# Tokens 0 to 511 in rows of 128, the first x tile and DFT block in halves, and VectorE normalising for all four early tiles

## The chip, the cores and the metric

The kernel runs on one core of a Trainium2 chip. The metric is device time in microseconds (us). All times of a trace count from the start of the profiled span.

## The reference

`x` has 2048 tokens of 512 features. It is normalised by layer norm; of the result a two-dimensional Fourier mixing and a gated linear unit are computed; the two are multiplied, after a silu on the second.

```python
xn = _layernorm(A_x)                                    # (1, 2048, 512)
a, b = xn @ dft_hid_re.T, xn @ dft_hid_im.T
s = dft_seq_re @ a - dft_seq_im @ b                     # 2048x2048 each
h = _sigmoid(xn @ w_gate) * (xn @ w_up)                 # 512 -> 1792
return A_x + s * _silu(h @ w_down)                      # 1792 -> 512
```

## The kernel before

**Arithmetic.** Every matrix product is made of fp32r matmuls on a high and a low part of each operand. ScalarE (ACT) copies a raw page into the high part (`Parts.high`, L118), VectorE (DVE) subtracts it from the raw page to get the low part (`Parts.make`, L123), and `mm3` (L70) issues three matmuls for one product: high x high, and the two mixed ones. On top of that the large products are cut into 2x2 blocks and done with seven block products in place of eight; the sums for it are DVE work (`combine`, L127).

**Units.** The work of TensorE (PE) is a list of units. The first 24 are the only ones the change touches directly: for k = 1 and 2, for four token tiles pp = 0 to 3, for three chunks t = 0 to 2 of 512 output rows of the sequence DFT, one unit `Chunk.run(k, pp)` of 12 matmuls of 128x512. Units 0 to 11 have k = 1, units 12 to 23 k = 2; in each group units 0 to 2 are tile 0, 3 to 5 tile 1, and so on. Chunk t writes the PSUM banks `ga`/`ua`, `gb`/`ub` or `gc`/`uc`, so the names in the rows tell the chunk. Each unit needs its own DFT block (a page of 128x1024 fp32, 512 KB, from `in_c_re`), split in two parts, and half of the token tile (128x512), normalised and split in two parts, which three units share.

**A token tile.** `fetch(j, pp)` loads a page with 256 of a block of 512 tokens; j = 0 serves k = 1, and j = 1 serves k = 2. `stats(j, pp)` takes mean and variance on DVE (L160, L161), adds epsilon there, raises to the power -0.5 on GpSimd (POOL, L164 or L167) and multiplies to a bias on POOL (L173). `normalise(j, pp, d)` applies scale and bias on ACT in place (L179): `d = 0` or `1` is one half of the features, no `d` the whole page. For tiles 0 and 1 of j = 0 `begin` does it another way (`prepare`): the powers are taken for one token of the pair at a time (`apart`), and DVE subtracts the mean and multiplies by the power (`normed`, L392), ACT splits the half at once (`high`, L395), DVE makes the low part (`low`, L398).

**Order.** The order on each engine is the order in which the program issues. Before unit n come the calls registered with `sooner(n, ...)`, then loads up to 5 units ahead, then the splits of the operands up to 2 units ahead, then `amid(n, ...)`, the unit's matmuls, and `after(n, ...)`. `begin` issues the very first work by hand: 15 matmuls on ones that warm up PE, the first loads, and the splits for the first units. All loads go through SP's queue.

Much later, `x_norm` (L457) applies the stored means and scales to the transposed x for the gated unit, 512 tokens at a time, on DVE; its operand is read from DRAM, where `store_moments` put it.

Of the kernel before, what the change touches and what calls it, by code (L numbers as in the profile page):

```python
# [32 lines left out]
def fnet_glu_kernel(ctx: ExitStack, tc: tile.TileContext, x, x_t, c_re, c_im, w_h, w_gu, w_down, out):  # L33
# [115 lines left out]
    def fetch(j, pp):  # L149
        xs[j, pp] = page([2, D], F32)  # L150
        rows = x[pp * SB : (pp + 1) * SB, :].rearrange("(p j e) d -> p j e d", j=2, e=2)[:, j]
        nc.sync.dma_start(xs[j, pp], rows)

    def stats(j, pp, apart=None):
        mv = stat.tile([P, 2, 2], F32, name="mv")
        rs = stat.tile([P, 2], F32, name="rs")
        mean, scale, bias = (moments[:, pp, m, j, :] for m in range(3))
        for e in range(2):
            st = stat.tile([P, 6], F32, name="st")
            nc.vector.bn_stats(st, xs[j, pp][:, e, :])  # L160
            nc.vector.bn_aggr(mv[:, e, :], st)  # L161
            if apart:
                nc.vector.tensor_scalar(rs[:, e : e + 1], mv[:, e, 1:2], EPS, None, op0=ALU.add)
                nc.gpsimd.tensor_tensor(scale[:, e : e + 1], rs[:, e : e + 1], mhalf[:, e : e + 1], op=ALU.pow)  # L164
        if not apart:
            nc.vector.tensor_scalar(rs, mv[:, :, 1], EPS, None, op0=ALU.add)
            nc.gpsimd.tensor_tensor(scale, rs, mhalf, op=ALU.pow)  # L167
        if apart:
            apart(mv, 0)
        nc.vector.tensor_scalar(mean, mv[:, :, 0], -1.0, None, op0=ALU.mult)  # L170
        if apart:
            apart(mv, 1)
        nc.gpsimd.tensor_tensor(bias, mean, scale, op=ALU.mult)  # L173
        return mv

    def normalise(j, pp, d=None):
        for e in range(2):
            v = xs[j, pp][:, e, :] if d is None else a_block(d, j, pp)[:, e]
            nc.scalar.activation(v, v, AF.Identity, scale=moments[:, pp, 1, j, e : e + 1], bias=moments[:, pp, 2, j, e : e + 1])  # L179

    def store_moments(b):
        nc.gpsimd.dma_start(m_part[b], moments[:, b, 0:2].rearrange("p m j e -> p m (j e)"))
# [45 lines left out]
    class Chunk:  # L228
# [34 lines left out]
        def run(self, k, pp):  # L263
# [4 lines left out]
            order = [(d, e) for d in range(2) for e in range(2)]  # L268
            if (k, pp) == (1, 0) and self.t < TOGETHER:
                order.sort(key=lambda v: v[1])  # L270
            split_up = self.t < TOGETHER and k in (1, 2)
            for lows in ((0,), (1,), (2,)) if split_up else ((0, 1, 2),):
                for d, e in order:
                    ws = [v[:, e, d * P : (d + 1) * P] for v in wv]
                    first, last = k in (1, 5) and pp == e == 0, pp == 3 and e == 1
                    mm3(self.ps[ch, d], ws, [v[:, e, :] for v in xv], first, last, k not in (1, 5), self.t > 0 or (k < 3 and pp > 0), lows)
# [52 lines left out]

    def begin_seq():  # L330
# [34 lines left out]
    def begin(chunks):  # L365
        for i, tag in enumerate(("gb", "ub", "pd", "pd")):
            idle = bank(tag)
            for _ in range((4, 4, 4, 3)[i]):
                nc.tensor.matmul(idle, ones[:, :P], ones, start=True, stop=True)
        c = chunks[0].op[1, 0]  # L370
        raw = c.loads[0]
        fetch(0, 0)
        raw.load()
        for n in (1,):
            units[n][0][1].load()
        fetch(0, 1)
        for n in (2, 3, 4):
            units[n][0][1].load()
        fetch(0, 2)
        for n in (5,):  # L380
            units[n][0][1].load()
        c.at = page([2, SB]), page([2, SB])

        def tile_of(pp):
            a = aop[1, pp]
            both = page([2, 2, D // 2])
            a.at = both[:, 0], both[:, 1]
            return a.at, a_block(0, 0, pp)

        def normed(pp, mv, e):  # L390
            v = a_block(0, 0, pp)[:, e]
            nc.vector.tensor_scalar(v, v, mv[:, e, 0:1], moments[:, pp, 1, 0, e : e + 1], op0=SUB, op1=ALU.mult)  # L392

        def high(parts, src, e):
            nc.scalar.activation(parts[0][:, e], src[:, e], AF.Copy)  # L395

        def low(parts, src, e=slice(0, 2)):
            nc.vector.tensor_tensor(parts[1][:, e], src[:, e], parts[0][:, e].bitcast(F32), op=SUB)  # L398

        def prepare(pp, between):  # L400
            parts, src = tile_of(pp)

            def step(mv, e):
                normed(pp, mv, e)
                high(parts, src, e)
                between(e)

            stats(0, pp, step)
            return parts, src
# [37 lines left out]
    def x_norm(h, b, at):  # L447
# [448 lines left out]
def _layout(inputs):  # L896
    import numpy as np

    def seq(c):
        c = np.asarray(c).reshape(NT, SB, 4, P, 2, 2)  # L900
        return np.ascontiguousarray(c.transpose(0, 4, 2, 3, 5, 1))
# [41 lines left out]
```

## Time and profile before

| | |
|---|---|
| runs of the kernel | 803.99, 804.27, 808.01 us; median 804.27 us |
| the profiled execution | 803.3 us, of which the span is 801.5 us |
| PE | 790.1 us busy (99%), 3471 matmuls |
| DVE | 686.5 us busy (86%) |
| ACT | 513.1 us busy (64%) |
| POOL | 119.2 us busy (15%) |
| granted TensorE clock | 1.00 |

A row of the timeline has the start, the duration, engine, line, operation, output and input, and how many equal instructions it merges; in brackets stand the engine's idle time just before it and what ended that. A row of the windows has busy time and, in brackets, the number of instructions of each engine in that stretch. A row of the waits has the total, the number of waits and the longest one.

### The profile page before, as it was taken

What the parts mean: (1) busy time and instruction counts of PE and PEld (TensorE: products, weight loads), DVE (VectorE), ACT (ScalarE), POOL (GpSimd) and SP (SyncE); (2) the same over time, 40 slices, a digit from 0 to 9 for tenths busy, and PEclk for the clock granted to TensorE, in tenths of its full rate; (3) what the DMA queues carried; (4) which work ended last, traced back from release to release, by engine and by line L of the source; (5) the groups of instructions that cost most, each with busy time, mean ns of one, the idle gap of its engine ahead of it and who ended that gap; (6) DMA issues with size and microseconds to landing.
All of it is one profiled execution on the core that took longest, in us unless ns stands there. A gap on an engine that the chain in (4) does not pass through costs nothing.

```text
span 801.5 us, 9883 instructions
## 1 busy us (share of the span) xinstructions
PE 790.1 (99%) x3471; PEld 650.3 (81%) x3471; DVE 686.5 (86%) x899; ACT 513.1 (64%) x785; POOL 119.2 (15%) x161
## 2 busy tenths in 40 slices
PE   8999999999999999999999999999999999999997
PEld 6777888888888888888887887888888888888886
DVE  6789999878899798899999967869688898896957
ACT  5686665525434555677777866666577787887571
POOL 1330001000110000001211111222131111112201
PEclk9999999999999999999999999999999999999999
DMA  9944047288799336228976976799999798999996
GB/s 352 418 176 157 27 156 291 79 311 292 264 377 383 105 110 202 84 113 213 205 130 98 178 162 190 248 267 245 240 262 212 158 228 228 223 291 309 299 333 106
DMA packets 49185, 174.72 MB, mean 218 GB/s; under 512 B 5488, under 2 KB 5744, under 8 KB 49136
## 3 DMA queue, kind: packets, MB, share of 16 engines
q0 software_dynamic: 20320, 70.28, 39.7%
q1 hardware_dynamic: 28736, 103.76, 35.4%
q8 instruction: 27, 0.44, 0.2%
q14 instruction: 22, 0.18, 0.1%
q10 hardware_dynamic: 80, 0.07, 0.0%
HBM read 106.95 MB, written 70.80 MB: 222 GB/s over the span
## 4 chain that ended last, share of the span: by engine, by line
PE 85%; DVE 5%; issue 4%; DMA 3%; ACT 1%; POOL 1%; POOLq 0%; DVEq 0%; ACTq 0%
PE pd L70 25%; PE ga L70 15%; PE ua L70 15%; PE gc L70 10%; PE uc L70 10%; PE gb L70 5%; PE ub L70 5%; DMA g_part<-page 2%; DVE page L123 2%; DVE page L127 1%; DVE st L160 1%; ACT page L118 1%; DMA page<-in_x_dram 1%; POOL g_part L499 1%; ACT page L179 0%
## 5 line engine op out<-in xcount | busy, mean ns | idle before, releaser
L123 DVE TENSOR_TENSOR page<-page 128x1024 fp32r<-128x1024 f32 (+1 forms) x383 | 348.1, 940 | 63.6 <-ACT page L118 61.6
L118 ACT ACTIVATE page<-page 128x1024 fp32r<-128x1024 f32 (+1 forms) x383 | 302.3, 830 | 143.1 <-DVE page L127 122.5
L70 PE MATMUL pd<-page 128*128 128x512 f32 (+1 forms) x984 | 238.0, 387 | 0.0
L70 PEld LDWEIGHTS pd<-page 128*128 128x128 f32 x984 | 183.2, 188 | 37.5
L127 DVE TENSOR_TENSOR page<-page 128x1024 f32<-128x1024 f32 (+2 forms) x252 | 204.5, 834 | 2.5 <-DMA page<-in_w_gu_dram 1.5
L70 PE MATMUL ga<-page 128*128 128x512 f32 x600 | 156.6, 391 | 2.6 <-ACT page L395 1.2
L70 PE MATMUL ua<-page 128*128 128x512 f32 x600 | 155.5, 389 | 0.0
L70 PEld LDWEIGHTS ga<-page 128*128 128x128 f32 x600 | 112.1, 188 | 29.3 <-ACT page L395 2.2
L70 PEld LDWEIGHTS ua<-page 128*128 128x128 f32 x600 | 112.7, 188 | 23.4
L70 PE MATMUL gc<-page 128*128 128x512 f32 x408 | 106.8, 389 | 0.0
L70 PE MATMUL uc<-page 128*128 128x512 f32 x408 | 106.7, 389 | 0.0
L499 POOL DMA_DIRECT2D g_part<-page x76 | 65.4, 861 | 277.2 <-ACT page L508 160.8
L508 ACT ACTIVATE page<-pd 128x512 f32<-128x512 f32 x140 | 81.7, 599 | 25.5 <-PE pd L70 18.1
L70 PEld LDWEIGHTS gc<-page 128*128 128x128 f32 x408 | 76.5, 188 | 16.1 <-DVE page L123 0.2
L70 PEld LDWEIGHTS uc<-page 128*128 128x128 f32 x408 | 76.6, 188 | 15.9
L70 PE MATMUL gb<-page 128*128 128x512 f32 x228 | 61.3, 391 | 1.7 <-DVE page L123 1.7
L70 PE MATMUL ub<-page 128*128 128x512 f32 x228 | 61.0, 389 | 0.0
L70 PEld LDWEIGHTS gb<-page 128*128 128x128 f32 x228 | 42.5, 188 | 11.7 <-DVE page L123 3.1
L70 PEld LDWEIGHTS ub<-page 128*128 128x128 f32 x228 | 42.8, 188 | 8.9
L281 POOL DMA_DIRECT2D f_raw<-page x16 | 8.7, 542 | 207.8 <-DVE page L293 145.8
L634 DVE TENSOR_TENSOR page<-page 128x512 f32<-128x512 f32 x28 | 19.3, 690 | 8.7 <-ACT page L631 7.9
L594 DVE TENSOR_TENSOR page<-page,pd 128x512 f32<-128x512 f32 x28 | 18.5, 684 | 6.9 <-PE pd L70 6.9
(86 smaller groups left out, 352.3 us busy)
## 6 DMA issues: line engine op xcount, KB each, us to landing
g_part<-page POOLq DMA_DIRECT2D x84, 512.0 KB, 6.9
page<-in_c_re_dram SPq DMA_DIRECT2D x48, 512.0 KB, 8.2
page<-in_c_im_dram SPq DMA_DIRECT2D x32, 512.0 KB, 6.7
page<-f_raw SPq DMA_DIRECT2D x28, 512.0 KB, 7.8
page<-in_w_gu_dram SPq DMA_DIRECT2D x22, 512.0 KB, 6.7
f_raw<-page POOLq DMA_DIRECT2D x16, 512.0 KB, 5.1
f_sum<-page POOLq DMA_DIRECT2D x16, 512.0 KB, 7.3
page<-f_sum SPq DMA_DIRECT2D x16, 512.0 KB, 12.3
```

Of the source, the lines that this page charges most:

```text
L70: nc.tensor.matmul(ps, ws[w], ms[m], start=first and i == 0, stop=last and i == 2, skip_group_check=go_on)
L118: nc.scalar.activation(self.parts[0], self.raw, AF.Copy)
L123: nc.vector.tensor_tensor(lo, self.raw, hi.bitcast(F32), op=SUB)
L127: (engine or nc.vector).tensor_tensor(dst, a, b, op=op)
L160: nc.vector.bn_stats(st, xs[j, pp][:, e, :])
L281: nc.gpsimd.dma_start(f_raw[self.t][block], v)
L499: nc.gpsimd.dma_start(g_part[i], pg, accum_op=ADD)
L508: nc.scalar.activation(pg[:, o, :], po, AF.Copy, scale=float(sign))
L594: nc.vector.tensor_add(self.part[:, o, :], self.part[:, o, :], ps)
L634: nc.vector.tensor_mul(s[k][:, 0, :], s[k][:, 0, :], ps["u" + tag] if tag else s[k][:, 1, :])
```

## The change

1. **Tokens.** The 512 tokens of tile 0 are laid out in rows of 128 consecutive tokens: a page for tile 0 is fetched as two DMAs of 128x512, each a contiguous 256 KB, on its own semaphore. Their moments are stored transposed (`moment`), the DFT blocks of tile 0 are packed on the host in the same token order, and `x_norm` for these tokens reads its operand with the token row innermost, at a stride of four elements.
2. **First DFT block.** It is loaded as two halves of 256 KB, and its two high parts are issued on ACT after the high part of each half of the token tile; the low parts follow in the order tile half 0, block half 0, tile half 1, block half 1. Unit 0 runs its 12 matmuls half by half, with the tile's low part used before the block's.
3. **Tiles 2 and 3 of j = 0** are prepared as tiles 0 and 1 were: powers one token at a time, DVE normalises and ACT splits each half. This stands ahead of unit m - 2 (m is the tile's first unit) together with the high part of that unit's DFT block, instead of the statistics after unit m - 5 and the normalising on ACT ahead of unit m - 2.
4. **j = 1:** `normalise(1, pp)` is issued after unit m - 5 and no longer ahead of it.
5. All early units with k = 1 or 2 now issue their matmuls in three passes of four (high x high, tile's low, block's low), with the tile's low part before the block's; the DFT block of unit 2 is loaded before tile 1's x page; one warm-up matmul less.

```diff
-        rows = x[pp * SB : (pp + 1) * SB, :].rearrange("(p j e) d -> p j e d", j=2, e=2)[:, j]
-        nc.sync.dma_start(xs[j, pp], rows)
+        if pp == 0:
+            rows = x[:SB, :].rearrange("(e j p) d -> j p e d", j=2, e=2)[j]
+        else:
+            rows = x[pp * SB : (pp + 1) * SB, :].rearrange("(p j e) d -> j p e d", j=2, e=2)[j]
+        if e is None and pp:
+            nc.sync.dma_start(xs[j, pp], rows)
+        else:
+            for i in range(2) if e is None else (e,):
+                nc.sync.dma_start(xs[j, pp][:, i, :], rows[:, i, :])
...
+    def moment(pp, m, j):
+        return moments[:, 0, m, :, j] if pp == 0 else moments[:, pp, m, j, :]
...
-            order = [(d, e) for d in range(2) for e in range(2)]
-            if (k, pp) == (1, 0) and self.t < TOGETHER:
-                order.sort(key=lambda v: v[1])
-            split_up = self.t < TOGETHER and k in (1, 2)
-            for lows in ((0,), (1,), (2,)) if split_up else ((0, 1, 2),):
...
+            turns = [(d, e, (0, 1, 2)) for d in range(2) for e in range(2)]
+            if self.t < TOGETHER and k < 3:
+                turns = [(d, e, (i,)) for i in range(3) for d in range(2) for e in range(2)]
+                if (self.t, k, pp) == (0, 1, 0):
+                    turns.sort(key=lambda v: v[1])
+                elif (k, pp) == (1, 0):
+                    turns.sort(key=lambda v: (v[2], v[1]))
...
-                    sooner(m - 5, lambda pp=pp: normalise(1, pp))
+                    after(m - 5, lambda pp=pp: normalise(1, pp))
...
-                        after(m - 5, lambda pp=pp: stats(0, pp))
-                        sooner(m - 2, lambda pp=pp: normalise(0, pp, 0))
+                        sooner(m - 2, units[m][0][1].high)
+                        sooner(m - 2, lambda pp=pp: ready.append(prepare(pp)))
+                        amid(m - 2, lambda: low(*ready.pop()))
...
-            for _ in range((4, 4, 4, 3)[i]):
+            for _ in range((4, 4, 3, 3)[i]):
...
-        raw.load()
-        for n in (1,):
+        for e in range(2):
+            nc.sync.dma_start(raw.at[:, e, :], raw.src[:, e, :])
+        for n in (1, 2):
             units[n][0][1].load()
         fetch(0, 1)
...
-        high(c.at, raw.at, 0)
-        a, first = prepare(0, lambda e: high(c.at, raw.at, 1) if e == 0 else None)
+        a, first = prepare(0, lambda e: high(c.at, raw.at, e))
         for e in range(2):
+            low(a, first, e)
             low(c.at, raw.at, e)
-            low(a, first, e)
         units[1][0][1].get()
-        units[2][0][1].high()
-        a, second = prepare(1, lambda e: None)
+        units[2][0][1].get()
         units[3][0][1].high()
-        units[2][0][1].get()
+        a, second = prepare(1)
         low(a, second)
...
-            to = v.rearrange("k i (p o) -> k i p o", o=4)
-            by = both.load()[:, :, m, :].unsqueeze(1).to_broadcast([P, 2, P, 4])
+            by = both.load()[:, :, m, :]
+            if c == 0:
+                to, by = v.rearrange("k i (o p) -> k i o p", o=4), by.rearrange("k p o -> k o p").unsqueeze(1).to_broadcast([P, 2, 4, P])
+            else:
+                to, by = v.rearrange("k i (p o) -> k i p o", o=4), by.unsqueeze(1).to_broadcast([P, 2, P, 4])
```

The order of instructions at three places, first of the kernel before, then of the changed one. ACT at the start: `page` of 128x256 is a half of the token tile, 128x512 a half of the first DFT block, and 128x1024 the block of a later unit.

```order
L395 ACTIVATE page<-page 128x512
L395 ACTIVATE page<-page 128x256
L395 ACTIVATE page<-page 128x512
L395 ACTIVATE page<-page 128x256
L118 ACTIVATE page<-page 128x1024 x2
```

```order
L356 ACTIVATE page<-page 128x256
L356 ACTIVATE page<-page 128x512
L356 ACTIVATE page<-page 128x256
L356 ACTIVATE page<-page 128x512
L118 ACTIVATE page<-page 128x1024 x3
```

The first half of the DFT block has moved behind the first half of the tile.

ACT around units 7 to 9: 128x512 from `page,moments` is the first `normalise(1, pp)`, 128x1024 the high part of a DFT block.

```order
L179 ACTIVATE page<-page,moments 128x256 x2
L179 ACTIVATE page<-page,moments 128x512 x2
L118 ACTIVATE page<-page 128x512
L118 ACTIVATE page<-page 128x1024 x2
L179 ACTIVATE page<-page,moments 128x256 x2
```

```order
L118 ACTIVATE page<-page 128x1024 x2
L356 ACTIVATE page<-page 128x256 x2
L190 ACTIVATE page<-page,moments 128x512 x2
L118 ACTIVATE page<-page 128x1024
L190 ACTIVATE page<-page,moments 128x256 x2
```

`normalise(1, 0)` stood ahead of the tile's split and of two DFT blocks; now the tile's two splits and one DFT block that stood behind it come before it, and ACT's normalising (128x256) of tile 3's first half is gone.

DVE around units 4 to 9: a group from BN_STATS to the last TENSOR_SCALAR is one `stats`, 128x1024 is the low part of a DFT block, 128x512 that of a tile.

```order
L161 BN_AGGR mv<-st 128x2
L166 TENSOR_SCALAR rs<-mv 128x2
L170 TENSOR_SCALAR moments<-mv 128x2
L160 BN_STATS st<-page 128x6
L161 BN_AGGR mv<-st 128x2
L160 BN_STATS st<-page 128x6
L161 BN_AGGR mv<-st 128x2
L166 TENSOR_SCALAR rs<-mv 128x2
L170 TENSOR_SCALAR moments<-mv 128x2
L123 TENSOR_TENSOR page<-page 128x1024 x2
L123 TENSOR_TENSOR page<-page 128x512
L123 TENSOR_TENSOR page<-page 128x1024
```

```order
L177 TENSOR_SCALAR rs<-mv 128x2
L181 TENSOR_SCALAR moments<-mv 128x2
L123 TENSOR_TENSOR page<-page 128x1024 x2
L171 BN_STATS st<-page 128x6
L172 BN_AGGR mv<-st 128x2
L174 TENSOR_SCALAR rs<-mv 128x1
L171 BN_STATS st<-page 128x6
L172 BN_AGGR mv<-st 128x2
L174 TENSOR_SCALAR rs<-mv 128x1
L353 TENSOR_SCALAR page<-page,mv,moments 128x256
L181 TENSOR_SCALAR moments<-mv 128x2
L353 TENSOR_SCALAR page<-page,mv,moments 128x256
```

Two `stats`, of tile 3 (j = 0) and of tile 0 (j = 1), stood together ahead of two DFT blocks' low parts; now the two low parts stand between them, and tile 3's group has the two normalising instructions.

More of the change, by code (lines that the diff above doesn't have):

```diff
@@ L156, in stats @@
         rs = stat.tile([P, 2], F32, name="rs")
-        mean, scale, bias = (moments[:, pp, m, j, :] for m in range(3))
+        mean, scale, bias = (moment(pp, m, j) for m in range(3))
         for e in range(2):
@@ L327, in add_product, with tile_of, normed, high @@
                 add(self.needs(k, pp), lambda k=k, pp=pp: self.run(k, pp))
+    ready = []
+    def tile_of(pp):
+        a = aop[1, pp]
+        both = page([2, 2, D // 2])
+        a.at = both[:, 0], both[:, 1]
+        return a.at, a_block(0, 0, pp)
+    def normed(pp, mv, e):
+        v = a_block(0, 0, pp)[:, e]
+        nc.vector.tensor_scalar(v, v, mv[:, e, 0:1], moment(pp, 1, 0)[:, e : e + 1], op0=SUB, op1=ALU.mult)
+    def high(parts, src, e):
+        nc.scalar.activation(parts[0][:, e], src[:, e], AF.Copy)
+    def low(parts, src, e=slice(0, 2)):
+        nc.vector.tensor_tensor(parts[1][:, e], src[:, e], parts[0][:, e].bitcast(F32), op=SUB)
+    def prepare(pp, between=None):
+        parts, src = tile_of(pp)
+        def step(mv, e):
+            normed(pp, mv, e)
+            high(parts, src, e)
+            if between:
+                between(e)
+        stats(0, pp, step)
+        return parts, src
     def begin_seq():
```

49 lines of the change are left out of this document (16 added, 33 removed).

## The prediction

> **What bounds the kernel now.** I read the page first, then the busy time by windows, the waits of the early part, the chain of waits, and last the timeline of the first 80 us. In the page, PE is busy for 99% of the span and is 85% of the chain.
>
> ```profile
> PE 790.1 (99%) x3471; PEld 650.3 (81%) x3471; DVE 686.5 (86%) x899; ACT 513.1 (64%) x785; POOL 119.2 (15%) x161
> PE 85%; DVE 5%; issue 4%; DMA 3%; ACT 1%; POOL 1%; POOLq 0%; DVEq 0%; ACTq 0%
> ```
>
> So only time in which PE waits can be won. The windows show where that is: busy time of each engine by stretch, then the granted clock, the DMA share and GB/s.
>
> ```profile
> 0.00:8.34 8.34, 5.68 (x15) 4.22 (x16) 2.90 (x10) 2.59 (x5) 1.53 (x8) 1.00 0.75 256
> 8.34:17.01 8.67, 8.53 (x36) 6.53 (x37) 8.17 (x18) 5.31 (x8) 1.58 (x4) 1.00 1.02 419
> 17.01:41.50 24.49, 23.35 (x102) 18.71 (x101) 19.12 (x36) 16.58 (x26) 7.57 (x8) 1.00 1.03 419
> 41.50:78.20 36.70, 35.79 (x154) 27.95 (x153) 34.49 (x48) 26.20 (x38) 6.86 (x9) 1.00 0.45 156
> 78.20:200.00 121.80, 121.80 (x539) 100.85 (x538) 110.95 (x112) 66.40 (x84) 7.77 (x13) 1.00 0.55 193
> 200.00:400.00 200.00, 200.00 (x883) 165.32 (x882) 184.13 (x215) 115.07 (x165) 18.67 (x29) 1.00 0.63 206
> 78.56 10.89 PE pd L70 x48
> ```
>
> From 78.2 to 400 PE is never idle; the 24 early units, at 8.34 to 78.2, are not so dense. The last row, of the chain, gives a dense matmul: 10.89 us for 48, 0.227 us each. The 288 early matmuls would take 65.3 us and take 69.9, so at most 4.5 us can be won behind the first matmul, beside what makes that one start sooner. Everything the change moves but `x_norm` lies ahead of 78.2. After that PE is the chain, so what those units give up at 78 the end gives up too.
>
> **The first unit.** Timeline of the start:
>
> ```profile
> 5.04 2.10 PE L369 MATMUL pd<-ones 128*128 128x512 f32 x7
> 5.41 0.69 DVE L160 BATCH_NORM_STATS2 st<-page 128x6 f32<-128x512 f32 x1 [4.00 <-DMA page<-in_x_dram]
> 6.42 0.69 DVE L160 BATCH_NORM_STATS2 st<-page 128x6 f32<-128x512 f32 x1
> 6.72 0.63 ACT L395 ACTIVATE page<-page 128x512 fp32r<-128x512 f32 x1 [4.48 <-DMA page<-in_c_re_dram]
> 7.43 0.41 DVE L392 TENSOR_SCALAR page<-page,mv,moments 128x256 f32<-128x256 f32 x1
> 7.87 1.28 ACT L395 ACTIVATE page<-page 128x256 fp32r<-128x256 f32 x3 [0.52 <-DVE page L392]
> 8.29 0.41 DVE L392 TENSOR_SCALAR page<-page,mv,moments 128x256 f32<-128x256 f32 x1 [0.38 <-POOL moments L164]
> 8.34 0.19 PEld L70 LDWEIGHTS ga<-page 128*128 128x128 f32 x1 [1.63 <-ACT page L395]
> 11.56 0.19 PEld L70 LDWEIGHTS gb<-page 128*128 128x128 f32 x1
> ```
>
> The tile's page lets DVE start at 5.41 and the DFT block, one page behind, lets ACT start at 6.72: a page lands every 1.31 us. A half should land 0.65 earlier, so statistics begin at 4.76 in place of 5.41. The second group began 1.01 later: 5.77, and its half, due at 5.4, does not hold it. From there normalising is 1.01 later (6.78), the split 0.44 after that (7.22). The block's first high part is now behind the tile's: 0.42 and 0.62 with some 0.09 of overlap, 0.95, then 0.04 to PE: 8.21, against 8.34. So the start alone wins 0.13; the new order on ACT eats what the half DMA gave. But the operands then arrive in the order of use: unit 0 took 11.56 - 8.34 = 3.22 us with its waits and would take 12 x 0.227 + 0.11 (the slower first pair) = 2.83. Unit 1 begins at 11.04: **0.5 us won**. If the half lands no sooner (5.41 and 6.72 as for two pages), the second group starts at 6.73, the first matmul at 9.17 and unit 1 at 12.0: 0.44 lost. That is the lower bound, and with both halves 0.3 earlier the upper is 0.8 won. The smaller warm-up leaves PE idle from 6.9 instead of 7.14, for 1.3 us instead of 1.2, at a clock of 1.00 in the windows; I cost it at nothing.
>
> The Trainium skill, "DMA: Bandwidth & Descriptors", section "Bandwidth", asks for DMAs of 1 MiB or more, and "Anatomy of one DMA" gives a fixed cost of about 2.0 us each, which speaks against halves. The rows have pages 1.31 us apart in flight, so a fixed cost there is overlapped; paid in series (an estimate from that page) it would put the second half near 7.3 and unit 1 near 12.6.
>
> **The stalls.** The waits from 8 to 80 us name the cause, the timeline the places (rows of PE that only fill up are left out).
>
> ```profile
> ACT page L179 <- POOL moments L173: 11.1, 5, 3.2
> DVE page L123 <- ACT page L118: 6.6, 7, 2.2
> ...
> 27.78 0.69 DVE L160 BATCH_NORM_STATS2 st<-page 128x6 f32<-128x512 f32 x1
> 29.47 0.61 PE L70 MATMUL ub<-page 128*128 128x512 f32 x2
> 29.66 2.35 DVE L123 TENSOR_TENSOR page<-page 128x1024 fp32r<-128x1024 f32 x2
> 29.76 1.67 POOL L167 TENSOR_TENSOR moments<-rs,mhalf 128x2 f32<-128x2 f32 x1 [0.91 <-DVE moments L170]
> 30.93 0.73 PE L70 MATMUL gb<-page 128*128 128x512 f32 x2 [0.85 <-DVE page L123]
> 31.51 0.62 PE L70 MATMUL ub<-page 128*128 128x512 f32 x2
> 32.10 1.52 ACT L179 ACTIVATE page<-page,moments 128x512 f32<-128x512 f32 x2 [2.11 <-POOL moments L173]
> 33.53 2.51 ACT L118 ACTIVATE page<-page 128x512 fp32r<-128x512 f32 x3
> 34.24 0.61 PE L70 MATMUL uc<-page 128*128 128x512 f32 x2
> 35.15 0.73 PE L70 MATMUL ga<-page 128*128 128x512 f32 x2 [0.29 <-ACT page L118]
> 35.71 0.63 PE L70 MATMUL ua<-page 128*128 128x512 f32 x2
> ...
> 42.99 0.61 PE L70 MATMUL uc<-page 128*128 128x512 f32 x2
> 45.46 0.62 PE L70 MATMUL ua<-page 128*128 128x512 f32 x2
> ...
> 56.42 0.61 PE L70 MATMUL ub<-page 128*128 128x512 f32 x2
> 57.96 0.62 PE L70 MATMUL ub<-page 128*128 128x512 f32 x2
> 73.41 0.61 PE L70 MATMUL ub<-page 128*128 128x512 f32 x2
> 75.07 0.63 PE L70 MATMUL ub<-page 128*128 128x512 f32 x2
> ```
>
> Start to start less 0.227 per matmul gives five losses: (a) 29.47 to 31.51, four matmuls, 1.13; (b) 34.24 to 35.71, 0.56; (c) 42.99 to 45.46, eight matmuls, 0.65; (d) 56.42 to 57.96, 0.63; (e) 73.41 to 75.07, 0.75. Together 3.72.
>
> (a) DVE made two statistics in one run, the second from 27.78, and only then, at 29.66, the low part that unit 7 waited for: one statistics costs 29.66 - 27.78 = 1.88 us. Now tile 3's stand ahead of unit 7 and not behind unit 4, so the two low parts come between. I follow DVE in the new order. The first unit's four low parts end near 10.0; two low parts of blocks, spaced 1.13 (a pair takes 2.35, one 1.22), end at 12.3; `prepare` takes 8.29 + 0.41 - 5.41 = 3.3, I take 3.2 of it since a little of the 0.38 wait goes, to 15.5; the split and the tile's low part to 16.6, three blocks to 20.0, `prepare` 23.2, a block 24.3, the tile 24.9, statistics 26.8, a block's low part **28.0**. Unit 7 is reached at 11.04 + 6 x 2.72 = 27.4 and needs it in its third pass, at 29.2. So (a) goes, with 1.2 us to spare.
>
> Next late is tile 3's own low part: two blocks to 29.1, `prepare` 32.3, a block 33.4, the tile 34.1; unit 9 (reached at 32.8) wants it in its second pass at 33.7. So (b), where ACT stood at `normalise(1, 0)` for the powers from POOL and the splits queued behind it, becomes a wait of 0.4 for DVE.
>
> (c) is the same `normalise` for the next tile; it is now issued behind the splits of its unit, which no longer wait for POOL. Who waits for `normalise` itself is the k = 2 tile, units later. I take (c) as gone; bounds 0 and 0.65.
>
> (d) and (e) hang on DVE low parts behind statistics and sums whose order is unchanged. DVE has lost part of its 6.6 us of waits for ACT by then, so I leave 0.25 of (d) and 0.55 of (e); bounds nothing and all. Kept in sum: 0.4 + 0.25 + 0.55 = 1.2; **won 2.5**, between 1.5 and 3.7.
>
> What DVE takes over are four normalisings of 0.41, 1.64 us; ACT is rid of four, and busy far less than DVE in the windows. SP issues two more DMAs ahead of 8 us and two more for the j = 1 page of tile 0. Loads are ahead of their use; from 8 to 80 us one wait for a load is in the list, and it is short:
>
> ```profile
> ACT page L118 <- DMA page<-in_c_re_dram: 0.4, 1, 0.4
> ```
>
> **The sum.** 0.5 + 2.5 = 3.0 us. The profiled execution has 803.3 us (1.8 around its span), 1.0 under the median of 804.27; with 803.99 and 804.27 the mean is 803.85, and 803.85 - 3.0 gives **800.8**. On the profiled execution's own time it is 800.3. The bounds, -0.44 + 1.5 = 1.1 and 0.8 + 3.7 = 4.5, give 802.8 and 799.3.
>
> **Rivals.**
>
> *The halves come late.* If small DMAs land as pages do, 0.44 is lost at the start and 2.5 still won: 801.8. For it: the first DMA took from 0.7 to 5.4 us, far above the later spacing, so early DMAs are slow for another reason than their size. Against: the 1.31 us between two pages.
>
> *DVE becomes the bound.* From 8.34 to 78.2 it is busy 8.17 + 19.12 + 34.49 = 61.8 of 69.9 us. With 1.64 more it must be 95% busy if 3.0 are to be won. If its 8.1 us of idle stay, because they come from other waits than those for ACT, the stalls grow by 1.64, and with 0.5 won at the start the time is 805.0. It decides once less than 1.6 of the 6.6 us of waits go.
>
> *The strided operand.* `x_norm` for the first 512 tokens reads one operand at a stride of 16 bytes, in four instructions. No row has such a stride; the nearest are the same lines without it.
>
> ```profile
> L457 DVE TENSOR_TENSOR page<-page x16: 1215/1218/1223, 221.8 to 414.9; 128x1024 f32<-128x1024 f32 x16
> 235.46 2.44 DVE L123 TENSOR_TENSOR page<-page 128x1024 fp32r<-128x1024 f32 x2
> ```
>
> DVE is busy for 92% from 200 to 400, so nearly all of an excess would reach PE. At f times 1.22 us the cost is up to 4.9 (f - 1) us: from f = 1.6 it eats the gain, from f = 2.5 the kernel is over 4 us slower; f = 4 gives 800.8 + 14.6 = 815.4. This is the case on the slow side. "VectorE: DVE Perf Modes" of the Trainium skill, section "Mode 1x (REGULAR)", has one result a cycle for fp32 whatever the strides; by it f is 1, and no run here shows it yet.
>
> **How the numbers follow.** About 0.5%, 4 us, is what a measurement of this kernel can tell from no change. The forecast has 0.80: nearly all of its range stays within 4 us of 803.85, and 0.14 is for the corner where most of (b) to (e) goes and the halves are early (under 799.85). The late halves have 0.09, DVE as the bound 0.06, both within 0.5%; the stride 0.05, slower. So faster 0.14, same 0.81, slower 0.05. The range, 799.0 to 803.0, takes in the forecast's bounds and the late halves and leaves out DVE as the bound and the stride.
>
> **What would show it.** In the changed kernel's trace: the first BATCH_NORM_STATS2 near 4.8, the first real matmul near 8.2, unit 1 (`gb`) near 11.0; no wait of PE near 28 to 31; a wait of some 0.4 near 34 for the tile's low part (L359); none near 42 to 45; shorter ones near 54 and 71; the first `pd` matmul near 75.2 in place of 78.2; four L475 instructions still of 1.22 us. A first `gb` after 11.6, waits for DVE that add up to 3 us or more, or an L475 above 2 us would make the forecast wrong.

## The result and the profile after

The changed kernel takes 803.09 us (median of 17 runs) and the kernel before 804.50 us in the same comparison. The ratio is 0.9977, with a 95% interval of 0.9966 to 0.9988: about 1.9 us won, which is within 0.5%. The forecast was 800.8 / 803.85 = 0.9962. On the forecast's base of 803.85 the measured ratio gives 802.0, inside the range of 799.0 to 803.0 and 1.2 us above the forecast; the median itself, 803.09, stands just above that range. The two profiled executions lie closer together than the medians, 803.3 and 802.94 us.

The small difference hides two large ones. The engine line of the page and the busy time by windows of the changed kernel, its windows cut at its own first matmul and at its own first `pd` matmul:

```profile
PE 789.2 (99%) x3470; PEld 649.5 (81%) x3470; DVE 691.5 (86%) x905; ACT 511.9 (64%) x783; POOL 118.9 (15%) x163
```

```profile
7.01:17.01 10.00, 10.00 (x44) 8.12 (x44) 8.47 (x17) 6.50 (x10) 1.39 (x3) 1.00 0.99 388
17.01:41.50 24.49, 24.17 (x105) 19.21 (x104) 23.21 (x47) 17.08 (x27) 7.34 (x10) 1.00 1.03 419
41.50:74.08 32.58, 32.39 (x143) 26.12 (x141) 31.20 (x44) 22.96 (x32) 6.86 (x9) 1.00 0.51 183
74.08:200.00 125.92, 125.92 (x557) 104.20 (x556) 115.09 (x115) 67.86 (x85) 8.31 (x14) 1.00 0.53 188
200.00:400.00 200.00, 198.24 (x875) 163.75 (x874) 185.57 (x216) 115.58 (x168) 18.12 (x28) 1.00 0.64 206
```

In the early part PE now idles 0.32 + 0.19 us behind 17; before it was 1.14 + 0.91. The stretch from 200 to 400, which was never idle, now has 1.76 us of idle time. The first weight load of `pd` marks the end of the early units, first in the kernel before, then in the changed one:

```profile
78.16 0.52 PEld L70 LDWEIGHTS pd<-page 128*128 128x128 f32 x2
```

```profile
74.08 0.89 PEld L70 LDWEIGHTS pd<-page 128*128 128x128 f32 x4
```

So 4.08 us are won by then, where the forecast had 3.0. Later 1.8 of them are lost at one place, and in the profiled execution most of the rest between 480 and 540 us. These are PE's waits over the whole span of the changed kernel (total, number, longest), and the rows of the timeline around the longest:

```profile
PE ga L70 <- DVE page L123: 1.8, 1, 1.8
PE gb L413 <- DVE ones L50: 1.5, 1, 1.5
PE ga L70 <- ACT page L634: 1.3, 2, 0.8
PE ga L70 <- ACT page L356: 0.6, 1, 0.6
PE pd L70 <- ACT page L526: 0.5, 1, 0.5
PE ga L70 <- DVE page L359: 0.3, 1, 0.3
PE gb L70 <- DVE page L123: 0.2, 1, 0.2
```

```profile
217.72 2.10 DVE L475 TENSOR_TENSOR page<-page 128x1024 f32<-128x1024 f32 x1
...
228.89 2.13 DVE L475 TENSOR_TENSOR page<-page 128x1024 f32<-128x1024 f32 x1
230.94 2.34 DVE L127 TENSOR_TENSOR page<-page 128x1024 f32<-128x1024 f32 x2
233.21 2.42 DVE L123 TENSOR_TENSOR page<-page 128x1024 fp32r<-128x1024 f32 x2
234.47 1.20 PE L70 MATMUL ga<-page 128*128 128x512 f32 x4 [1.76 <-DVE page L123]
```

L413 is the warm-up, L475 is `x_norm`. Two of its four strided instructions stand ahead of the low part that PE waits for, each some 0.9 longer than the 1.22 of the other twelve; 2 x 0.9 is the wait.

The start of the changed kernel, as before:

```profile
3.56 0.69 DVE L171 BATCH_NORM_STATS2 st<-page 128x6 f32<-128x512 f32 x1 [2.16 <-DMA page<-in_x_dram]
4.58 0.68 DVE L171 BATCH_NORM_STATS2 st<-page 128x6 f32<-128x512 f32 x1
6.02 1.81 ACT L356 ACTIVATE page<-page 128x256 fp32r<-128x256 f32 x4 [3.79 <-DVE page L353]
7.01 0.19 PEld L70 LDWEIGHTS ga<-page 128*128 128x128 f32 x1 [1.05 <-ACT page L356]
9.67 0.19 PEld L70 LDWEIGHTS gb<-page 128*128 128x128 f32 x1
```

Statistics begin at 3.56 (before 5.41, forecast 4.76), the first matmul at 7.01 (8.34, forecast 8.21), and unit 1's weights at 9.67 (11.56 before).

Last, who waits for whom from 7 to 80 us, of DVE for ACT and of ACT for POOL:

```profile
DVE page L123 <- ACT page L118: 1.7, 3, 0.9
ACT page L190 <- POOL moments L184: 1.1, 1, 1.1
```

Before, these two were 6.6 and 11.1 us. Of the five stalls two places are left, rows of PE:

```profile
32.60 0.63 PE L70 MATMUL ua<-page 128*128 128x512 f32 x2
33.55 0.73 PE L70 MATMUL ga<-page 128*128 128x512 f32 x2 [0.32 <-DVE page L359]
34.12 0.62 PE L70 MATMUL ua<-page 128*128 128x512 f32 x2
...
69.59 0.61 PE L70 MATMUL ub<-page 128*128 128x512 f32 x2
70.40 0.73 PE L70 MATMUL gb<-page 128*128 128x512 f32 x2 [0.19 <-DVE page L123]
70.97 0.62 PE L70 MATMUL ub<-page 128*128 128x512 f32 x2
```

From start to start less 0.227 per matmul, 0.61 is lost at 33.55, for tile 3's low part (L359), and 0.47 is left of (e) at 70.40. (a), (c) and (d) are gone.

### The profile page after: what moved, and what is told of

It reads as the page before. It is cut to its first block, busy times and chain, and to the rows that moved or that the text cites. A ratio compares the mean times of both kernels' runs of the same rounds, so it can differ in the third digit from the quotient of the medians.

```text
span 801.2 us, 9892 instructions
## 1 busy us (share of the span) xinstructions
PE 789.2 (99%) x3470; PEld 649.5 (81%) x3470; DVE 691.5 (86%) x905; ACT 511.9 (64%) x783; POOL 118.9 (15%) x163
## 4 chain that ended last, share of the span: by engine, by line
PE 74%; DVE 13%; issue 5%; DMA 4%; ACT 1%; POOL 1%; SPq 0%; DVEq 0%; POOLq 0%; ACTq 0%
PE pd L70 21%; PE ga L70 13%; PE ua L70 13%; PE gc L70 9%; PE uc L70 9%; DVE page L123 6%; PE gb L70 5%; PE ub L70 5%; DVE page L127 4%; DMA g_part<-page 2%; DMA w_part<-page 2%; DVE page L475 1%; DMA page<-in_c_re_dram 1%; DVE st L171 1%; DVE page L652 1%
## 5 line engine op out<-in xcount | busy, mean ns | idle before, releaser
L118 ACT ACTIVATE page<-page 128x1024 fp32r<-128x1024 f32 (+1 forms) x381 | 301.7, 831 | 153.6 <-DVE page L127 128.8
L123 DVE TENSOR_TENSOR page<-page 128x1024 fp32r<-128x1024 f32 (+1 forms) x381 | 347.1, 943 | 55.9 <-ACT page L118 54.2
L127 DVE TENSOR_TENSOR page<-page 128x1024 f32<-128x1024 f32 (+2 forms) x252 | 205.0, 836 | 5.9 <-DMA page<-in_w_gu_dram 5.1
```

The costliest lines, as they stand in the source:

```text
L118: nc.scalar.activation(self.parts[0], self.raw, AF.Copy)
L123: nc.vector.tensor_tensor(lo, self.raw, hi.bitcast(F32), op=SUB)
L127: (engine or nc.vector).tensor_tensor(dst, a, b, op=op)
```

## The experiments

Each ratio is to the kernel before on the same chip. The first four separate the late loss from the early gain, and in the early gain the halves from the token rows.

### The scales stored packed

The changed kernel, but the scales and means of the first 512 tokens are written to DRAM transposed, so that `x_norm` reads them without a stride.

```diff
-        nc.gpsimd.dma_start(m_part[b], moments[:, b, 0:2].rearrange("p m a b -> p m (a b)"))
+        to = m_part[b] if b else m_part[b].rearrange("m o p -> p m o")
+        nc.gpsimd.dma_start(to, moments[:, b, 0:2].rearrange("p m a b -> p m (a b)"))
...
-                to, by = v.rearrange("k i (o p) -> k i o p", o=4), by.rearrange("k p o -> k o p").unsqueeze(1).to_broadcast([P, 2, 4, P])
+                to, by = v, both.load()[:, m, :].unsqueeze(1).to_broadcast([P, 2, SB])
```

> The changed kernel with the moments of tokens 0 to 511 written to DRAM transposed, so that x_norm reads them contiguously; nothing else. Theory A (the wait of 1.9 us at 234 comes from the strided operand alone): the four L475 go from 2.1 back to 1.22 us, the wait at 234 falls to 0.1 us, and the time is 1.8 us under the changed kernel, a ratio to before of about 0.9955. Rival B (DVE is late at 234 because its work stands otherwise since the first 80 us): the instructions are shorter but a wait of 1 us or more stays, and less than 0.9 us is won. Rival C (time won ahead of 400 us is given back at 490 to 530, where PE waits for sums loaded from DRAM): the wait at 234 goes, but the waits at 490 to 530 grow by as much and the ratio stays at 0.9977.

Measured: 800.07 us (6 runs) against 804.39, ratio 0.9946 (0.9932 to 0.9959), 800.04 us in the profiled execution. The line of `x_norm` (minimum, median and maximum in ns, first and last start), in the changed kernel and in this one:

```profile
L475 DVE TENSOR_TENSOR page<-page x16: 1214/1221/2143, 217.7 to 412.7; 128x1024 f32<-128x1024 f32 x16
```

```profile
L477 DVE TENSOR_TENSOR page<-page x16: 1216/1219/1223, 217.7 to 410.9; 128x1024 f32<-128x1024 f32 x16
232.12 1.77 PE L70 MATMUL ga<-page 128*128 128x512 f32 x6
```

The long instructions are gone, and PE passes the place where it had waited 1.76 without an idle time in the row. The stride cost the changed kernel its 1.8 us at this place, as theory A has it. The waits near 494 and 527 did not grow in return (rival C): PE's waits for ACT there and near 435 fell from 1.8 to 1.2 us in all. The profiled spans differ by more, 801.2 and 798.3 us, and the part beyond 1.8 and these waits was not followed up. The ratio lies below those of both other kernels, outside their intervals.

### The strided operand alone

The kernel before, with the operand of `x_norm` for the first 512 tokens read at a stride of four elements. The token rows and the stored moments stay as they were, so these tokens get the moments of others: the run is for the time alone.

```diff
+            if c == 0:
+                to = v.rearrange("k i (o p) -> k i o p", o=4)
+                by = both.load()[:, :, m, :].rearrange("k p o -> k o p").unsqueeze(1).to_broadcast([P, 2, 4, P])
```

> The kernel before with the four x_norm instructions of the first 512 tokens reading their operand at a stride of four elements (which gives these tokens wrong moments); nothing else. Theory A: four L457 of 2.1 us, a wait of PE of 1.9 us near 239, and 1.8 us more than before, a ratio of 1.0022. Rival B: instructions longer, but PE waits less than 0.9 us for them. Rival C: 1.8 us are lost at 239 and won back in smaller waits at 490 to 530; ratio 1.000.

Measured: 806.51 us (8 runs) against 804.39, ratio 1.0025 (1.0014 to 1.0037). The line of `x_norm`, and the wait of PE that the kernel before does not have:

```profile
L460 DVE TENSOR_TENSOR page<-page x16: 1206/1220/2137, 221.9 to 416.9; 128x1024 f32<-128x1024 f32 x16
```

```profile
PE ga L70 <- DVE page L123: 1.8, 1, 1.8
```

The same price, 2.1 in place of 1.22 us, and the same wait of 1.8, put into a kernel that had none of the rest. With the experiment above it stands from both sides.

### Whole pages in the new token rows

The changed kernel with its halved loads made whole again.

```diff
-        if e is None and pp:
+        if e is None:
...
-        for e in range(2):
-            nc.sync.dma_start(raw.at[:, e, :], raw.src[:, e, :])
+        nc.sync.dma_start(raw.at, raw.src)
```

> The changed kernel with each of the three halved loads (two x pages of tile 0 and the first DFT block) as one DMA again; the token rows stay contiguous. Theory H (the half is what lands early): the first statistics begin near 5.4 as before, the first real matmul near 8.9, 1.9 us later than in the changed kernel, and most of that reaches the end: ratio near 1.000. Rival K (contiguous token rows are what makes the early load fast): the statistics begin near 4.2 and the first matmul near 7.7, 0.7 us later than in the changed kernel; ratio near 0.9985.

### Halves in the old token rows

The kernel before with the first x page and the first DFT block loaded in two halves each, and nothing else.

```diff
-        nc.sync.dma_start(xs[j, pp], rows)
+        if (j, pp) == (0, 0):
+            for i in range(2):
+                nc.sync.dma_start(xs[j, pp][:, i, :], rows[:, i, :])
+        else:
+            nc.sync.dma_start(xs[j, pp], rows)
...
-        raw.load()
+        raw.at = page(raw.shape, F32)
+        for e in range(2):
+            nc.sync.dma_start(raw.at[:, e, :], raw.src[:, e, :])
```

> The kernel before with the first x page and the first DFT block loaded as two halves each, tokens in their old rows (each half then takes rows of 2 KB at a pitch of 8 KB); order of instructions as before. Theory H: the first statistics begin near 3.6, the first real matmul near 6.6, unit 1 near 9.8 (11.56 before); the low parts on DVE for the later units move with it, so that up to 1.8 us stays at the first pd matmul: ratio near 0.998. Rival K: with the pitch of 8 KB a half lands near 4.6 to 5, the first matmul near 7.6 to 8, and under 0.8 us is won: ratio 0.999 to 1.000.

Measured: whole pages 803.52 us (12 runs), ratio 0.9990 (0.9979 to 1.0000); halves in the old rows 803.94 us (11 runs), ratio 0.9991 (0.9983 to 1.0000), both against 804.39. The first statistics, whole pages first, then halves:

```profile
4.44 0.69 DVE L171 BATCH_NORM_STATS2 st<-page 128x6 f32<-128x512 f32 x1 [3.04 <-DMA page<-in_x_dram]
```

```profile
4.23 0.69 DVE L164 BATCH_NORM_STATS2 st<-page 128x6 f32<-128x512 f32 x1 [2.83 <-DMA page<-in_x_dram]
```

With 5.41 before and 3.56 after these make a table of two by two: halving brings 1.18 in the old rows and 0.88 in the new ones, the new rows bring 0.97 for a page and 0.67 for a half. The eight kernels here whose first load is the contiguous half begin between 3.28 and 3.77, so an entry is good to some 0.5. Within that, each step by itself is about as large as the 0.65 that the forecast gave to both together, or larger. The first matmul came at 7.89 with whole pages, near rival K's 7.7, and at 7.42 with the halves in the old rows, between the two theories: neither the size nor the rows do it alone.

What the start is worth later is another matter. With whole pages the first matmul came 0.88 later than in the changed kernel, but the first `pd` at 74.43 only 0.35 later; in time the two are not told apart. The halves in the old rows won 0.92 at the first matmul and still had them at `pd` (77.25), and the profiled execution ended no earlier than that of before. These are two of its waits, of ACT from 205 to 240 us, and of PE over the span:

```profile
ACT page L118 <- DMA f_raw<-page: 4.2, 1, 4.2
```

```profile
PE ga L70 <- DVE page L123: 0.8, 1, 0.8
```

ACT stood 4.2 us for a page on its way through DRAM, DVE was then idle 0.76 behind ACT's split, and PE waited 0.8 for the low part, at a place where the kernel before has no idle time in its rows. PE arrived 0.9 earlier, but ACT got the page only at 228.59, in the kernel before at 227.57. Why this transfer ended later was not tried.

### Items 3 and 4 of the change taken back

The other five kernels start from the version with the packed scales (first `pd` at 74.11). In the first three, tiles 2 and 3 or the j = 1 normalising or both are put back:

```diff
-                    after(m - 5, lambda pp=pp: normalise(1, pp))
+                    sooner(m - 5, lambda pp=pp: normalise(1, pp))
```

```diff
-                        sooner(m - 2, units[m][0][1].high)
-                        sooner(m - 2, lambda pp=pp: ready.append(prepare(pp)))
-                        amid(m - 2, lambda: low(*ready.pop()))
+                        after(m - 5, lambda pp=pp: stats(0, pp))
+                        sooner(m - 2, lambda pp=pp: normalise(0, pp, 0))
```

Both diffs (items 3 and 4 undone):

> The version with the stored scales packed (first pd matmul at 74.11 us, 800.07 us), with items 3 and 4 of the change undone: tiles 2 and 3 are prepared and the j = 1 pages normalised in the old places and on the old engines; the start, the three passes and the token rows stay. Theory S (the stalls were their own cause): the new start brings only what the kernel with the old token rows and halves brought at 78, 0.9, at most the 1.3 of the changed kernel's first matmul, and stalls (a) to (e) come back: first pd at 76.8 to 77.3, of which 1.1 at (a) near 30; time 802.6 to 803.2. Rival T (order of arrival): the start and the three passes alone bring the 4.1 at 78, since everything behind unit 0 only inherits its lateness: first pd within 0.5 of 74.11, time 800.1 to 800.6.

The first diff (item 4 undone):

> The version with the stored scales packed, with item 4 alone undone: normalise(1, pp) is issued ahead of unit m - 5 again. Theory S: stall (c) comes back (0.65 at 42.99 to 45.46) with part of (d) (0.63): first pd 0.7 to 1.3 later than 74.11, 74.8 to 75.4, nothing near 30; time 800.8 to 801.4. Rival: the stalls hang on item 3 alone, because the splits of tiles 2 and 3 no longer stand behind ACT's normalising: first pd within 0.3 of 74.11, no change of the time.

The second diff (item 3 undone):

> The version with the stored scales packed, with item 3 alone undone: the statistics of tiles 2 and 3 stand behind unit m - 5 again and ACT normalises them; normalise(1, pp) stays behind unit m - 5. Theory S: stall (a) comes back, 1.1 near 30 (two statistics in one run on DVE, 1.88, ahead of the low part of unit 7's block); the wait of 0.6 near 33.5 for tile 3's low part goes, and four normalisings of 0.41 leave DVE: first pd 0.5 to 1.1 later than 74.11, time 800.6 to 801.2. Rival: all of the 2.5 behind the start hangs on this item: first pd near 76.6, time 802.5.

Measured, in one comparison against 804.47 us; the last two columns are the waits from 7 to 80 us:

| put back | time, ratio | first `pd` | DVE for ACT (L123, L118) | ACT for POOL |
|---|---|---|---|---|
| both | 803.24, 0.9989 (0.9979 to 0.9998) | 76.93 | 6.3 | 11.5 |
| item 4 | 801.19, 0.9961 (0.9947 to 0.9974) | 75.66 | 3.2 | 3.5 |
| item 3 | 800.51, 0.9957 (0.9944 to 0.9969) | 75.12 | 4.9 | 6.2 |
| none | 800.07, 0.9946 (0.9932 to 0.9959), earlier comparison | 74.11 | 1.6 | 1.1 |

The stalls come back each with its own item. With both put back, (a), in the timeline of PE and, ahead of it, of DVE:

```profile
26.54 0.69 DVE L171 BATCH_NORM_STATS2 st<-page 128x6 f32<-128x512 f32 x1
28.42 2.35 DVE L123 TENSOR_TENSOR page<-page 128x1024 fp32r<-128x1024 f32 x2
29.70 0.73 PE L70 MATMUL gb<-page 128*128 128x512 f32 x2 [1.29 <-DVE page L123]
```

The second of two statistics stands ahead of the low part again, 1.88 of it, and PE waits 1.29. With item 3 alone put back the wait is there too, 1.3, and beside the warm-up's it is the only wait for DVE in PE's list:

```profile
PE gb L70 <- DVE page L123: 1.3, 1, 1.3
```

With none put back (d) is absent and (e) has 0.22 of idle time; with item 4 alone put back (a) is absent, and (d) and (e) are there with 0.34 and 0.44:

```profile
54.87 0.72 PE L70 MATMUL gb<-page 128*128 128x512 f32 x2 [0.34 <-DVE page L123]
71.97 0.73 PE L70 MATMUL gb<-page 128*128 128x512 f32 x2 [0.44 <-DVE page L123]
```

(c) is less clear: with both items put back 0.29 of it is back and another 0.37 stands near 47; with item 4 alone there is nothing at its place and 0.31 a unit and a half later. So (a) belongs to the place of the statistics, and (d) and half of (e) to `normalise(1, pp)`, with which ACT waited for POOL and DVE for ACT.

At `pd` item 3 is worth 76.93 - 75.66 = 1.27, item 4 76.93 - 75.12 = 1.81, and both 2.82; the rest, 78.16 - 76.93 = 1.23, is the start. (The three passes are no part of it: the kernel before had them in all 24 units, and of item 5 only the order inside units 0 and 12 is new.) Item 4's 75.66 lies above the 74.8 to 75.4 that was expected. These are single executions, and DVE did not stand alike in them: its first statistics of tile 1 begin at 10.95 with both put back, at 11.89 with item 4, at 12.05 with item 3, and at 11.65 with none. Counted from there, `pd` comes 65.98, 63.77, 63.07 and 62.46 us later, in the kernel before 66.53, so that both items together are worth 3.52 and the start 0.55. Which count is nearer to the truth is open; by both, the rivals (the start brings it all; all hangs on one item) are out. In time, each single item differs from none by less than the intervals tell apart.

### Who is first on DVE for tile 3

The wait at 33.55 was tried in two ways. First, the tile's low part is issued directly behind its normalising:

```diff
-                        sooner(m - 2, lambda pp=pp: ready.append(prepare(pp)))
-                        amid(m - 2, lambda: low(*ready.pop()))
+                        sooner(m - 2, lambda pp=pp: low(*prepare(pp)))
```

> The version with the stored scales packed, with the low parts of tiles 2 and 3 issued on DVE directly behind their normalising instead of behind the low part of the next DFT block (amid). Theory S: the wait for tile 3's low part at 33.55 (0.49 + 0.11) goes, first pd 73.5 to 73.8, time 799.5 to 799.8. Rival: DVE has no slack there, so that the block's low part behind it is late by the same 0.6 or more and PE waits there: first pd 74.1 to 74.7, time 800.1 to 800.7.

Measured: 800.91 us, ratio 0.9966 (0.9954 to 0.9979), first `pd` at 74.71, 0.6 later than without. The rival holds, by another cost than it named. DVE now waits for the split of the tile itself (total, number, longest):

```profile
DVE page L360 <- ACT page L357: 1.5, 3, 0.5
```

Without this edit that wait is 0.5, once: the block's low part that stood between had covered ACT's time. PE's wait only changes its place, 0.63 at 32.91 in place of 0.49 at 33.59.

Then the order on DVE is kept, and PE uses the block's low part ahead of the tile's in units 6 and 9:

```diff
-                mm3(self.ps[ch, d], ws, [v[:, e, :] for v in xv], first, last, k not in (1, 5), self.t > 0 or k < 3, only)
+                mm3(self.ps[ch, d], ws, [v[:, e, :] for v in xv], first, last, k not in (1, 5), self.t > 0 or k < 3 and (k, pp) not in ((1, 2), (1, 3)), only)
```

> The version with the stored scales packed, with the DFT block's low part again ahead of the tile's low part in the matmuls of the first units of tiles 2 and 3 (units 6 and 9); the order on DVE stays. Theory S (the wait of 0.49 + 0.11 at 33.59 is for tile 3's low part, which ends on DVE some 1.1 after the block's low part, and is only needed one pass later now): the wait goes, first pd 73.5 to 73.7, time 799.4 to 799.7. Rival: DVE is the bound from 20 to 74 (dense behind 34), so that what is won at 33.59 is lost again at the next low part (70.4, 0.38 + 0.11 now): first pd within 0.2 of 74.11, time unchanged.

Measured: 799.78 us against 803.88, ratio 0.9944 (0.9928 to 0.9961), first `pd` at 73.37, 0.74 earlier. The wait near 33.6 is gone, which looks like the theory; its time is not told apart from the version without this edit. But DVE was ahead before units 6 and 9 begin. Tile 1's first statistics, without the edit and with it:

```profile
11.65 0.69 DVE L171 BATCH_NORM_STATS2 st<-page 128x6 f32<-128x512 f32 x1
```

```profile
10.92 0.69 DVE L171 BATCH_NORM_STATS2 st<-page 128x6 f32<-128x512 f32 x1
```

That is 0.73 of the 0.74, and nothing up to there is changed by the edit. Five of the kernels have the same order on DVE up to `pd`, and in all five `pd` keeps its distance to these statistics, whatever PE's start was:

| kernel | unit 1's weights | tile 1's statistics | first `pd` | from statistics to `pd` |
|---|---|---|---|---|
| changed | 9.67 | 11.62 | 74.08 | 62.46 |
| scales packed | 9.86 | 11.65 | 74.11 | 62.46 |
| whole pages | 10.55 | 11.97 | 74.43 | 62.46 |
| stride of 8 bytes (below) | 10.09 | 11.48 | 73.92 | 62.44 |
| packed, block's low part first | 10.00 | 10.92 | 73.37 | 62.45 |

So the edit is not shown to win anything at `pd`, and the rival, with DVE as the bound, fits: without the lead of 0.73, `pd` would be at 74.10. Nor does the missing wait near 33.6 say much for the edit: with that lead, tile 3's low part ended at 32.79, and the weights of the second pass were loaded from 32.67, so that in the old order some 0.1 to 0.2 of the wait would have been left (an estimate from these two times). What sets DVE's place is a load. These are pieces at the start of the chain of the changed kernel that ended last (start, duration, what):

```profile
3.08 6.28 DMA page<-in_c_re_dram
9.38 1.07 ACT page L118
10.47 1.23 DVE page L123
11.70 0.61 DVE st L171
```

The block of unit 2 lands at 9.4 there, and its low part now stands ahead of tile 1's statistics. With this edit that ACT instruction begins at 8.68; why the block landed sooner in that execution is not known.

In the profiled execution the lead is lost again, part of it at 232, where PE waits 0.4 for a low part behind ACT's 3.8 us for the same transfer as above (0.8 and 4.2 with the halves in the old rows), the rest near 523.

### A stride of 8 bytes

```diff
-                to, by = v, both.load()[:, m, :].unsqueeze(1).to_broadcast([P, 2, SB])
+                for a in range(2):
+                    to = v.rearrange("k i (a c p) -> k i a c p", a=2, c=2)[:, :, a]
+                    by = both.load()[:, m, a].rearrange("k p c -> k c p").unsqueeze(1).to_broadcast([P, 2, 2, P])
+                    nc.vector.tensor_tensor(to, to, by, op=(ADD, ALU.mult)[m])
```

> The version with the stored scales packed, but laid out so that the operand of x_norm for the first 512 tokens is read at a stride of 8 bytes in place of 4 (16 in the changed kernel); each of the four instructions is made in two of 128x512. At 4 bytes such a 128x512 is 0.61 to 0.69, at 16 bytes 128x1024 was 2.12, half of it 1.06. Theory A1 (any stride above one element costs the same): 1.06 each. Theory A2 (the price grows with the stride): 0.7 to 0.9. Theory A3 (8 bytes is free): 0.69.

Measured in a single run: 801.02 us. The line of `x_norm` for these tokens:

```profile
L477 DVE TENSOR_TENSOR page<-page x8: 682/684/685, 217.6 to 244.0; 128x512 f32<-128x512 f32 x8
```

684 ns, as a 128x512 without a stride (0.68 to 0.69 in L127 and L123), which is theory A3. At 8 bytes the stride is free, at 16 it is not.

## Why the prediction was right or wrong

**The size of the whole** was right (no change that exceeds 0.5%), but by luck in part, as the difference of two terms that were both off: 4.1 won against 3.0, and 1.8 lost at a place that the sum did not have. The premise that the end gives up what the early units give up holds in part: in the profiled executions, the 4.05 that the kernel with packed scales is ahead at `pd` are 3.2 at 540, and of the 0.91 of the halves in the old rows nothing is left at the end.

**The first unit: the term that was mis-sized.** The step that failed is "a half should land 0.65 earlier". It took the spacing of two pages in flight as the time of a page, and gave nothing to the rows becoming contiguous. Measured it is 5.41 - 3.56 = 1.85. The path behind it was right: from the first statistics to the first matmul the forecast had 8.21 - 4.76 = 3.45, the trace has 7.01 - 3.56 = 3.45; "start alone 0.13" became 1.33 only through the landing. Unit 0 then took 2.66 for 2.83, and unit 1 won 1.89 and not 0.5. The sum carries this to the end in full, and that is not so: tile 1's statistics, to which `pd` keeps its distance in the five kernels above, begin at 11.62 in place of 11.63. What the start won on DVE went into the low part of unit 2's block, which now stands ahead of them, and into waiting for ACT and the loads. With the tiles left in their old places, unit 1 began 2.10 earlier and `pd` 1.23. The rival that halves come late fell with the landing. The second statistics, at 4.58, waited for nothing (with the halves in the old rows for 0.17, at 5.50). The estimate from the Trainium skill ("DMA: Bandwidth & Descriptors", "Anatomy of one DMA", a section on DMAs issued by GpSimd), with its fixed cost paid in series, had put their half near 7.3, so that cost is not paid in series by these loads on SP's queue.

**(a)** was right in cause and place: two statistics in one run ahead of unit 7's low part. Putting item 3 back restores it.

**Tile 3's low part** was right: a wait of 0.4 near 34 was forecast, 0.61 came at 33.55. That the order of the passes exposes it is not shown: the kernel before had the same order in these units, and in the kernel that turns it round DVE was 0.73 ahead for another reason.

**(c)** is gone as forecast; that `normalise(1, pp)` alone caused it is not shown, since it does not return at its place with that call.

**(d) and (e)**: the step "hang on DVE low parts behind statistics and sums whose order is unchanged" failed. They hung on `normalise(1, pp)` too, through the waits of ACT for POOL and of DVE for ACT. The forecast kept 0.25 and 0.55 of them; (d) kept nothing and (e) 0.47. The stalls' term, 2.5, came out at 4.08 - 1.89 = 2.19 as the sum counts it, behind unit 1's weights, and at 2.82 or 3.52 by putting both items back.

**DVE becomes the bound** did not happen as the rival had it, with stalls that grow by 1.64: its condition was that less than 1.6 of the 6.6 us of DVE's waits for ACT go, and 4.9 went. But DVE, with ACT and a load ahead of it, now sets the end of the early units: `pd` follows tile 1's statistics to within 0.02 in five kernels, and 31.20 busy of 32.58 us in the last of the early windows is 96%.

**The strided operand**, given 0.05, is what took nearly half of the gain. Its price came out at f = 2.12 / 1.22 = 1.74, just above the 1.6 that the rival named as the point that eats the gain. It did not eat all: of the four instructions' 3.6 us only the two ahead of 234 reached PE, 1.8; behind the other two DVE had room. "Nearly all of an excess would reach PE" was too much by a factor of two. "VectorE: DVE Perf Modes" of the Trainium skill, section "Mode 1x (REGULAR)", gives one result a cycle for this mode and names fp32 and odd strides among what it takes, with no exception. By the traces the price is the same at 4 and 8 bytes and 1.74 times that at 16, and here the measurement decides. The error was to rest so small a chance on a rule that no row here showed.

**What stays open.** Between 480 and 540 the profiled execution of the changed kernel gives back most of what the stride had left: the same ACT instruction on `pd` begins at 476.67 against 478.88 in the kernel before, 2.2 ahead, later at 514.64 against 516.22, and at 540.25 against 540.70, 0.45 ahead. PE waits for ACT near 494 (0.85, before 0.36) and 527 (0.53, before nothing). With packed scales 4.0 becomes 3.2. ACT waits for partial results from DRAM at these places; which transfer is late and why was not tried.

## What to carry to other kernels

A row of the trace that carries an instruction's price carries it for its access pattern: when an edit changes the order of data in memory, follow every later reader of that data and price its stride by a run, here 0.9 us for each of four instructions 200 us behind the edit. Time won early is kept only as far as DMA and the engines that are off the path come earlier as well; look for the next place where PE is ahead of a load, and, before crediting an edit with an earlier end, for an instruction on another engine that was already ahead where the edit begins. When an engine waits in a chain (POOL, ACT, DVE, PE), moving the first waiting instruction behind the work of others removes stalls that seem to belong to the last one.

## What the runs showed of the hardware

**Strides on DVE.** An fp32 TENSOR_TENSOR of 128x1024 with one operand at 16 bytes took 2.10 to 2.14 us, at 4 bytes 1.22; a 128x512 at 8 bytes took 0.684, as one at 4 bytes. Where between 8 and 16 bytes it turns, and whether it grows beyond, was not tried.

**The first loads.** With nothing else in flight ahead of them, the first statistics began at 5.41 for a page of 512 KB taken from every other pair of token rows, at 4.44 for a page of two contiguous blocks of 256 KB, at 4.23 for half a page in the old rows and at 3.56 for one contiguous block, each time the first DMA of the kernel. Executions with that same contiguous block spread from 3.28 to 3.77. Within this, the size of the first transfer and the order of its rows in memory matter about as much, 0.9 to 1.2 and 0.7 to 1.0 us.
